# One row group of the output weight split over fewer DMA engines, and a shorter VectorE program, in a one-token decoder block

## The chip, the cores and the metric

The kernel runs on one core of a Trainium2 chip. The metric is device time in microseconds (us) for one execution. Below, "span" is the stretch that the hardware profiler records on the core, from its first to its last instruction; the device time is somewhat longer.

## The reference, cut to what matters

One token (a row of D = 1024 numbers) goes through an attention layer over a sliding window of a cache and, beside it, through a two-layer network; both start from the same normalised row, and the sum of both and of the input is the result.

```python
x  = A_x                                   # 1 x 1024
xn = layernorm(x)
# A: attention, 32 query heads, 4 key/value heads, the last W = 4096 of 65536 cache rows, Dh = 128
q  = (xn @ wq)                             # wq 1024 x 4096, 32 heads x 128
p  = softmax(q . k[-4096:] * 128**-0.5)    # 8 query heads share one k/v head
A  = (p @ v[-4096:]).reshape(4096) @ wo    # wo 4096 x 1024
# B: the network
h  = gelu(layernorm(xn) @ w1 + b1)         # w1 1024 x 3584
B  = h @ w2 + b2                           # w2 3584 x 1024
out = x + A + B                            # bf16, 1024 numbers
```

All inputs are bf16. Every weight and the used part of the cache are read once: k 4 MB, wq 8 MB, w1 7 MB, v 4 MB, w2 7 MB and wo 8 MB.

## The kernel before, in words

**Loads.** SyncE (SP) issues all large loads on one queue, in the order k_sb (4 pieces), wq (2), w1 (2), v_sb (3), w2 (2), wo (6 pieces, L228), and at the end the store of the result (L357). The tiles come from a ring of four 32 KB-per-partition buffers, so a load waits until the engines have finished with the tile that held its buffer. `wo` is seen as 128 partitions x 32 "rows": partition p holds the rows 32p to 32p+31 of the matrix, and row (or chunk) c of the kernel is the 128 x 1024 slab of row 32p+c over all p. The chunks 0 to 15 come with one load, the others with loads of 8, 4, 2, 1 and 1 chunks; the last two are chunk 30 and chunk 31.

**Start.** The input row is turned into a column by eight one-column matmuls (x_ps, L123); the two layer norms (L124 to L170) are a chain of small VectorE (DVE) instructions with matmuls against a matrix of ones for the sums and a power on GpSimd (POOL) for the reciprocal root. They give xnT and yT. DVE also zeroes the accumulators accq (L174) and acch (L246).

**Keys.** DVE transposes k in 32 x 32 blocks into kt_scr (L185, four instructions of 128 x 4096), and 64 copies of 32 x 1024 put the blocks in place in kT: 26 on ScalarE (ACT, L199), 38 on DVE (L201).

**TensorE (PE).** In order: q = xn @ wq into accq (L237); the first half of acch = y @ w1 (L257); the transpose of q (L261), which DVE copies into the mask tile qm (L266); the scores sp (L275); the second half of acch; softmax (L283 to L305); gelu (L312) and the transpose hT of its result (L314); o_all = p @ v (L319). DVE reduces o_all (L322, L324), casts it to o_bf (L326), and four matmuls with the selection matrix `spread` lay it out over 128 partitions as o8 (L329, L331), one column for each chunk of wo.

**End.** The rest is one long sum over 28 chunks of w2 (with hT) and 32 chunks of wo (with o8). All but the last TAIL = 8 chunks go into accf (L338), two matmuls of 512 columns a chunk. The last 8 go into another accumulator, acct (L353), four matmuls of 256 columns a chunk, one in each group of 32 columns of the array. When the last matmul into accf is done, four copies of 1 x 256 bring accf into the tile bulk, alternately on DVE (L348) and ACT (L350). They all write the same tile, and each waits for the one before it on the other engine. DVE then adds acct and bulk (res, L356), and SP stores res.

```python
    TAIL = 8
...
    for t in range(4):
        half, w = divmod(t, 2)
        src = accf[32 * half:32 * half + 1, 256 * w:256 * w + 256]
        if w == 0:
            nc.vector.tensor_copy(out=bulk[32 * t:32 * t + 1, :], in_=src)
        else:
            nc.scalar.copy(out=bulk[32 * t:32 * t + 1, :], in_=src)
```

The order on each engine is the order of the program; a scheduler moves independent instructions a little.

Of the kernel before, what the change touches and what calls it, by code (L numbers as in the profile page):

```python
# [16 lines left out]
def kernel(  # L17
# [21 lines left out]
    Hq = NQ // Dh  # L39
    REP = Hq // Hkv  # L40
    Fd = B_w1.shape[1]
    W = min(4096, max(256, Sk // 4))
    C = D // P
    NCH = W // P
    NJQ = NQ // 512
    WQ4 = W // 4
    CW2 = Fd // P
    CWO = NQ // P
    TAIL = 8
    NH = Fd // 8  # L50
    eps = 1e-5
# [3 lines left out]
    consts = ctx.enter_context(tc.tile_pool(name="consts", bufs=1))  # L55
# [28 lines left out]
    for i in range(2):  # L84
# [6 lines left out]

    ident = consts.tile([P, P], BF16)
# [3 lines left out]
    ones_f = consts.tile([P, P], FP32)  # L96
    nc.vector.memset(ones_f[:], 1.0)
    sel4 = consts.tile([P, Hq], FP32)
    ones_bf = consts.tile([P, 1], BF16)
    nc.vector.memset(ones_bf[:], 1.0)  # L100
    mhalf = consts.tile([P, 1], FP32)
    nc.vector.memset(mhalf[:], -0.5)
    dummy = consts.tile([1, 2], FP32)
    nc.scalar.activation(out=dummy[:, 0:1], in_=mhalf[0:1, 0:1], func=ACT.Exp)  # L104
    qm = consts.tile([P, Hkv, Hq], BF16)
    nc.gpsimd.memset(qm[:], 0.0)

# [3 lines left out]
                            pattern=[[-1, 4], [1, P]], channel_multiplier=-4)  # L111

# [11 lines left out]
    nc.vector.tensor_copy(out=xf[:], in_=x_ps[:])  # L124

    def layernorm(src_f32, dst_f32, dst_bf):
        n = float(P * C)
        st = small.tile([P, 1], FP32, tag="ln_st")
        nc.vector.reduce_sum(out=st[:], in_=src_f32, axis=AX.X)
# [8 lines left out]
        nc.vector.tensor_tensor(out=sq[:], in0=xc[:], in1=xc[:], op=ALU.mult)  # L138
        nc.vector.reduce_sum(out=st2[:], in_=sq[:], axis=AX.X)
# [6 lines left out]
        nc.vector.tensor_scalar_mul(out=dst_f32, in0=xc[:], scalar1=rstd[:])  # L146
        nc.vector.tensor_copy(out=dst_bf, in_=dst_f32)

    xn_f = consts.tile([P, C], FP32)
    xnT = consts.tile([P, C], BF16)  # L150
    layernorm(xf[:], xn_f[:], xnT[:])
    n_el = float(P * C)
    st12 = small.tile([P, 2], FP32, tag="ln2_st")
    nc.vector.reduce_sum(out=st12[:, 0:1], in_=xn_f[:], axis=AX.X)
    sq2 = small.tile([P, C], FP32, tag="ln2_sq")
    nc.vector.tensor_tensor(out=sq2[:], in0=xn_f[:], in1=xn_f[:], op=ALU.mult)
    nc.vector.reduce_sum(out=st12[:, 1:2], in_=sq2[:], axis=AX.X)
# [28 lines left out]
    nc.vector.tensor_reduce(out=sel4[:], in_=ident_f[:].rearrange("p (r h) -> p h r", r=4), axis=AX.X, op=ALU.add)  # L186
    act_share = [11, 8, 5, 2]
    act_moves, dve_moves = [], []
    for g in range(Hkv):
        T4 = scr[:, g, :].rearrange("p (c a j) -> p c a j", a=4, j=32)  # L190
        k = 0
        for R in range(4):
            for Cd in range(4):
                src = T4[32 * R:32 * R + 32, :, Cd, :]
                dst = kT[32 * Cd:32 * Cd + 32, g, WQ4 * R:WQ4 * (R + 1)].rearrange("p (c j) -> p c j", j=32)
                (act_moves if k < act_share[g] else dve_moves).append((dst, src))
                k += 1
    for (dst, src) in act_moves:
        nc.scalar.copy(out=dst, in_=src)  # L199
    for (dst, src) in dve_moves:  # L200
        nc.vector.tensor_copy(out=dst, in_=src)  # L201
# [44 lines left out]
    nc.vector.memset(acch[:], 0.0)  # L246
# [15 lines left out]
    for g in range(Hkv):  # L262
        b, th = divmod(g, 2)
        src = qT_ps[:, b * 4:(b + 1) * 4, 64 * th:64 * th + 64:32]
        dst = qm[:, g, g * REP:(g + 1) * REP].rearrange("p (t hh) -> p hh t", t=2)
        nc.vector.tensor_copy(out=dst, in_=src)  # L266
# [38 lines left out]
    nc.vector.tensor_scalar_mul(out=grs[:], in0=gmask[:], scalar1=rs[:])  # L305
# [4 lines left out]
    nc.vector.tensor_scalar_mul(out=zcol[:], in0=l_loc[:], scalar1=0.0)  # L310
# [30 lines left out]
    nc.vector.memset(acct[:], 0.0)  # L341
# [9 lines left out]
    for idx, (kind, c, wap) in enumerate(chunk_src[n_bulk:]):  # L351
        for t in range(4):
            nc.tensor.matmul(acct[32 * t:32 * t + 1, :], lhsT=vec[kind](c), rhs=wap[:, t * 256:(t + 1) * 256],  # L353
                             start=(idx == 0), stop=(idx == TAIL - 1), tile_position=(0, 32 * t))
# [33 lines left out]
```

## Time and profile before

| | |
|---|---|
| device time, median of 3 runs | 102.2 us (101.95 to 102.44) |
| device time of the profiled execution | 102.15 us |
| its span | 100.4 us |
| bytes read from HBM | 39.86 MB, 397 GB/s over the span |
| busy share: PE, DVE, ACT, POOL | 45%, 49%, 34%, 4% |
| DVE, ACT, POOL, PE matmul instructions | 91, 37, 17, 369 |
| instruction fetches seen inside the span | 3 of 16 KB, 1 of 8 KB |

In the profile, `PE` rows are matmuls and `PEld` rows are loads of the stationary operand; `L338` is line 338 of the kernel above; a bracket such as `[0.54 <-DMA wo...]` says how long the engine sat idle before the instruction and what ended that. `PEclk` is the TensorE clock that was granted, 1.00 being full speed. `SPq` is SP's issuing of DMAs. Times in the views run from the start of the span.

### The profile page before, as it was taken

What the parts mean: (1) busy time and instruction counts of PE and PEld (TensorE: products, weight loads), DVE (VectorE), ACT (ScalarE), POOL (GpSimd) and SP (SyncE); (2) the same over time, 40 slices, a digit from 0 to 9 for tenths busy, and PEclk for the clock granted to TensorE, in tenths of its full rate; (3) what the DMA queues carried; (4) which work ended last, traced back from release to release, by engine and by line L of the source; (5) the groups of instructions that cost most, each with busy time, mean ns of one, the idle gap of its engine ahead of it and who ended that gap; (6) DMA issues with size and microseconds to landing.
All of it is one profiled execution on the core that took longest, in us unless ns stands there. A gap on an engine that the chain in (4) does not pass through costs nothing.

```text
span 100.4 us, 976 instructions
## 1 busy us (share of the span) xinstructions
PE 45.7 (45%) x369; PEld 18.0 (18%) x369; DVE 49.2 (49%) x91; ACT 34.2 (34%) x37; POOL 4.0 (4%) x17
## 2 busy tenths in 40 slices
PE   0472000009500920297462009999199910299640
PEld 0422000003100300024221003334133400033210
DVE  4616799999999999992552460000900000000310
ACT  2300008999999999902204630000000000000100
POOL 6024200000000000000000000000000000000000
PEclk9999999999999997559999655589957995559975
DMA  2999999999999998999999998989989999999900
GB/s 40 375 431 434 499 431 496 431 418 418 418 418 392 468 440 369 502 400 400 390 440 424 424 506 388 509 377 423 480 388 414 418 444 437 437 405 401 382 33 1
DMA packets 2882, 39.92 MB, mean 397 GB/s; under 512 B 311, under 2 KB 315, under 8 KB 702
## 3 DMA queue, kind: packets, MB, share of 16 engines
q1 hardware_dynamic: 2872, 39.85, 93.3%
q8 instruction: 3, 0.05, 0.2%
q10 hardware_dynamic: 6, 0.01, 0.0%
q14 instruction: 1, 0.01, 0.0%
HBM read 39.86 MB, written 0.00 MB: 397 GB/s over the span
## 4 chain that ended last, share of the span: by engine, by line
DVE 39%; DMA 25%; PE 15%; issue 8%; ACT 5%; POOL 3%; SPq 2%; POOLq 1%; ACTq 0%; DVEq 0%
DMA wo<-in_A_wo_dram 25%; DVE kt_scr L185 17%; DVE kT L201 16%; PE o_all L319 10%; PE sp L275 2%; DVE hT L314 2%; SPq L228 2%; PE acch L257 2%; ACT L312 1%; ACT e L297 1%; DVE eTb L299 1%; DVE m_loc L283 1%; ACT h_sb L312 1%; DVE q_sb L240 1%; POOLq L383 1%
## 5 line engine op out<-in xcount | busy, mean ns | idle before, releaser
L199 ACT COPY kT<-kt_scr 32x1024 bf16<-32x1024 bf16 x26 | 27.1, 1042 | 12.2 <-DVE kt_scr L185 12.0
L185 DVE STREAM_TRANSPOSE kt_scr<-k_sb 128x4096 bf16<-128x4096 bf16 x4 | 17.4, 4409 | 0.0
L201 DVE COPY kT<-kt_scr 32x1024 bf16<-32x1024 bf16 x38 | 15.9, 419 | 0.5
L237 PE MATMUL accq<-wq,xnT 128*1 128x512 bf16 x64 | 6.9, 607 | 19.5 <-DMA wq<-in_A_wq_dram 19.5
L350 ACT COPY bulk<-accf 1x256 f32<-1x256 f32 x2 | 0.7, 361 | 36.3 <-DVE bulk L348 36.3
L319 PE MATMUL o_all<-v_sb,eTb 128*32 128x512 bf16 x32 | 9.9, 484 | 5.4 <-DVE hT L314 5.4
L348 DVE COPY bulk<-accf 1x256 f32<-1x256 f32 x2 | 0.8, 416 | 21.6 <-PE accf L338 21.1
L338 PE MATMUL accf<-wo,o 128*1 128x512 bf16 x48 | 6.8, 449 | 6.5 <-DMA wo<-in_A_wo_dram 6.5
L338 PE MATMUL accf<-w,hT 128*1 128x512 bf16 x56 | 8.1, 452 | 0.1
L257 PE MATMUL acch<-w,yT 128*1 128x448 bf16 x64 | 4.8, 463 | 6.3 <-DMA w<-in_B_w_dram 6.3
L237 PEld LDWEIGHTS <-xnT 128*1 128x1 bf16 x64 | 2.1, 116 | 23.8 <-issue 23.8
L319 PEld LDWEIGHTS <-eTb 128*32 128x32 bf16 x32 | 3.7, 117 | 11.2 <-DVE hT L314 5.5
L322 DVE TENSOR_TENSOR o_m<-o_all,grs 32x512 f32<-32x512 f32 x1 | 0.7, 679 | 10.0 <-PE o_all L319 10.0
L338 PEld LDWEIGHTS <-o 128*1 128x1 bf16 x48 | 2.4, 94 | 10.9 <-issue 8.8
L338 PEld LDWEIGHTS <-hT 128*1 128x1 bf16 x56 | 2.8, 96 | 4.9 <-issue 2.7
L257 PEld LDWEIGHTS <-yT 128*1 128x1 bf16 x64 | 1.7, 99 | 9.0 <-issue 8.3
L314 DVE STREAM_TRANSPOSE hT<-h_sb 128x896 bf16<-128x896 bf16 x1 | 1.7, 1699 | 2.4 <-ACT h_sb L312 2.4
L297 ACT ACTIVATE e<-sc,nmx 128x1024 bf16<-128x1024 f32 x1 | 1.1, 1147 | 3.9 <-DVE nmx L294 3.9
L353 PE MATMUL acct<-wo,o 128*1 128x256 bf16 x32 | 1.7, 283 | 1.7 <-DMA wo<-in_A_wo_dram 1.7
L275 PE MATMUL sp<-kT,qm 128*32 128x512 bf16 x32 | 2.1, 380 | 0.3 <-DVE qm L266 0.3
L104 ACT ACT_TABLE_LOAD x1 | 1.3, 1283 | 1.9 <-issue 1.9
L299 DVE STREAM_TRANSPOSE eTb<-e 128x1024 bf16<-128x1024 bf16 x1 | 1.2, 1246 | 1.4 <-ACT e L297 1.4
(85 smaller groups left out, 32.2 us busy)
## 6 DMA issues: line engine op xcount, KB each, us to landing
w<-in_B_w_dram SPq DMA_DIRECT2D x4, 3584.0 KB, 23.7
wq<-in_A_wq_dram SPq DMA_DIRECT2D x2, 4096.0 KB, 19.9
k_sb<-in_A_k_cache_dram SPq DMA_DIRECT2D x4, 1024.0 KB, 7.0
wo<-in_A_wo_dram SPq DMA_DIRECT2D x1, 4096.0 KB
v_sb<-in_A_v_cache_dram SPq DMA_DIRECT2D x1, 2048.0 KB
v_sb<-in_A_v_cache_dram SPq DMA_DIRECT2D x2, 1024.0 KB, 22.5
wo<-in_A_wo_dram SPq DMA_DIRECT2D x1, 2048.0 KB, 21.6
wo<-in_A_wo_dram SPq DMA_DIRECT2D x1, 1024.0 KB
```

The lines of the kernel that those rows point to most:

```text
L185: nc.vector.transpose(out=scr[:, g, :], in_=k2[:, g, :])
L199: nc.scalar.copy(out=dst, in_=src)
L201: nc.vector.tensor_copy(out=dst, in_=src)
L228: nc.sync.dma_start(out=tv[:, a:b, :], in_=wo_v[:, nr * i + a:nr * i + b, :])
L237: nc.tensor.matmul(accq[32 * t:32 * t + 1, b, :], lhsT=xnT[:, c:c + 1], rhs=w3[:, r, j * 512:(j + 1) * 512], start=(c == 0), stop=(c == C ...
L257: nc.tensor.matmul(acch[32 * t:32 * t + 1, b, :NH], lhsT=yT[:, c:c + 1], rhs=w3[:, r, j * NH:(j + 1) * NH], start=False, stop=(c == C - 1) ...
L275: nc.tensor.matmul(sp[32 * R:32 * R + 32, :], lhsT=qm[:, g, :], rhs=kT[:, g, c0:c0 + 512], start=(g == 0), stop=(g == Hkv - 1), tile_posit ...
L297: nc.scalar.activation(out=e128[:], in_=sc[:], func=ACT.Exp, bias=nmx[:], scale=scale, accum_out=l_loc[:])
L299: nc.vector.transpose(out=eTb[:], in_=e128[:])
L314: nc.vector.transpose(out=hT[:], in_=h_sb[:].rearrange("p (d c) -> p c d", c=CW2))
L319: nc.tensor.matmul(o_all[:].rearrange("h g d -> h (g d)"), lhsT=eTb[:, 32 * c:32 * c + 32], rhs=v4[:, :, c, :], start=(c == 0), stop=(c == ...
L338: nc.tensor.matmul(accf[32 * half:32 * half + 1, :], lhsT=vec[kind](c), rhs=wap[:, half * 512:(half + 1) * 512], start=False, stop=(idx == ...
```

## The change

It has two parts.

First, chunk 30 of wo is no longer loaded by one DMA of 128 partitions. Its 128 slab rows are loaded by three DMAs: 48 rows to partitions 32 to 79 of the ring tile (wo_m), 48 rows to partitions 32 to 79 of a new tile wo_x, and 32 rows to partitions 0 to 31 of the ring tile. The source of each has 12, 12 or 8 as its outer dimension and 4 as its inner. Partitions 0 to 31 of wo_x are zeroed by POOL. Chunk 30 is then multiplied in two parts of 80 partitions each (8 matmuls instead of 4), and o8 gets two more columns, made by 8 one-column matmuls with a second selection matrix spread_x, that hold the matching order of o. TAIL becomes 4: accf takes 28 chunks of wo, acct four.

Second, DVE's 91 instructions become 44 (four of them only read out an accumulated sum). The 38 DVE copies into kT become 10, each over all four k/v heads (32 x 4 x 1024), and ACT does 24 copies, six of each head. The four copies into qm become 2, the four copies of the row maximum become part of one reduction, several sums are taken as the accumulated output of the instruction before, and memsets, casts, small products and zeroings move to POOL or ACT. POOL has 32 instructions instead of 17 (its first ones now also make the constants), ACT has a few more.

```diff
-    TAIL = 8
+    TAIL = 4
...
-        nc.vector.tensor_copy(out=dst_bf, in_=dst_f32)
+        nc.scalar.copy(out=dst_bf, in_=dst_f32)
...
-    nc.vector.tensor_tensor(out=msq2[:], in0=mean2[:], in1=mean2[:], op=ALU.mult)
+    nc.gpsimd.tensor_tensor(out=msq2[:], in0=mean2[:], in1=mean2[:], op=ALU.mult)
...
-    nc.vector.tensor_tensor(out=ve2[:], in0=ve2[:], in1=msq2[:], op=ALU.subtract)
+    nc.gpsimd.tensor_tensor(out=ve2[:], in0=ve2[:], in1=msq2[:], op=ALU.subtract)
...
+    MOVED = 30
+    moves = ((0, 32, 12, 0), (1, 32, 12, 48), (0, 0, 8, 96))
+    spread_x = consts.tile([Hq, 2, 4, P], BF16)
+    nc.gpsimd.memset(spread_x[:], 0.0)
+    for s, m0, ne, p0 in moves:
+        sx = spread_x[:, s, :, m0:m0 + 4 * ne].rearrange("h q (e v) -> h q e v", e=ne)
+        nc.gpsimd.affine_select(out=sx, in_=sx, compare_op=ALU.not_equal, fill=1.0, base=p0,
+                                pattern=[[-1, 4], [1, ne], [ne, 4]], channel_multiplier=-4)
+    wo_x = consts.tile([80, D], BF16)
+    nc.gpsimd.memset(wo_x[0:32, :], 0.0)
...
-    nc.vector.memset(accq[:], 0.0)
+    nc.scalar.mul(accq[:].rearrange("p b n -> p (b n)"), mhalf[:].to_broadcast([P, 1024]), 0.0)
...
-    act_share = [11, 8, 5, 2]
+    act_share = [6, 6, 6, 6]
...
+    for k, (R, Cd) in enumerate(pairs):
+        g0 = sum(k < share for share in act_share)
+        if g0 < Hkv:
+            nc.vector.tensor_copy(out=kT[32 * Cd:32 * Cd + 32, g0:, WQ4 * R:WQ4 * (R + 1)].rearrange("p g (c j) -> p g c j", j=32),
+                                  in_=T5[32 * R:32 * R + 32, g0:, :, Cd, :])
...
-            nc.sync.dma_start(out=tv[:, a:b, :], in_=wo_v[:, nr * i + a:nr * i + b, :])
+            if nr * i + a != MOVED:
+                nc.sync.dma_start(out=tv[:, a:b, :], in_=wo_v[:, nr * i + a:nr * i + b, :])
+                continue
+            wo_m = tv[0:80, a, :]
+            for s, m0, ne, p0 in moves:
+                rows = A_wo[p0 * CWO:(p0 + 4 * ne) * CWO, :].rearrange("(v e c) n -> e v c n", e=ne, c=CWO)
+                nc.sync.dma_start(out=(wo_m, wo_x)[s][m0:m0 + 4 * ne, :], in_=rows[:, :, MOVED, :])
...
-    nc.vector.memset(acch[:], 0.0)
+    nc.scalar.mul(acch[:].rearrange("p b n -> p (b n)"), mhalf[:].to_broadcast([P, 1024]), 0.0)
...
-    nc.vector.tensor_copy(out=o_bf[:], in_=o_f[:])
+    nc.scalar.copy(out=o_bf[:], in_=o_f[:])
...
+    for s in range(2):
+        for q in range(4):
+            nc.tensor.matmul(o8_ps[:, 32 + s:33 + s], lhsT=spread_x[:, s, q, :], rhs=o_bf[:, 32 * q + MOVED:32 * q + MOVED + 1],
+                             start=(q == 0), stop=(q == 3))
...
-        for t in range(4):
-            nc.tensor.matmul(acct[32 * t:32 * t + 1, :], lhsT=vec[kind](c), rhs=wap[:, t * 256:(t + 1) * 256],
-                             start=(idx == 0), stop=(idx == TAIL - 1), tile_position=(0, 32 * t))
+        parts = [(vec[kind](c), wap)]
+        if kind == "o" and c == MOVED:
+            parts = [(o8[0:80, 32:33], wo_m), (o8[0:80, 33:34], wo_x)]
+        for (lh, rh) in parts:
+            for t in range(4):
+                nc.tensor.matmul(acct[32 * t:32 * t + 1, :], lhsT=lh, rhs=rh[:, t * 256:(t + 1) * 256],
+                                 start=(idx == 0), stop=(idx == TAIL - 1), tile_position=(0, 32 * t))
```

More of the change, by code (lines that the diff above doesn't have):

```diff
@@ L89 @@
     kt_scr = ring_tile("kt_scr")
+    mhalf = consts.tile([P, 1], FP32)
+    nc.gpsimd.memset(mhalf[:], -0.5)
+    ones_bf = consts.tile([P, 1], BF16)
+    nc.gpsimd.memset(ones_bf[:], 1.0)
+    ones_f = consts.tile([P, P], FP32)
+    nc.gpsimd.memset(ones_f[:], 1.0)
     ident = consts.tile([P, P], BF16)
@@ L95 @@
     make_identity(nc, ident_f[:])
-    ones_f = consts.tile([P, P], FP32)
-    nc.vector.memset(ones_f[:], 1.0)
     sel4 = consts.tile([P, Hq], FP32)
[L99 to L102, printed above, removed]
     dummy = consts.tile([1, 2], FP32)
     nc.scalar.activation(out=dummy[:, 0:1], in_=mhalf[0:1, 0:1], func=ACT.Exp)
-    qm = consts.tile([P, Hkv, Hq], BF16)
+    qm = consts.tile([P, Hkv * (Hq + REP)], BF16)
     nc.gpsimd.memset(qm[:], 0.0)
-    spread = consts.tile([Hq, 4, P], BF16)
-    nc.gpsimd.memset(spread[:], 0.0)
-    nc.gpsimd.affine_select(out=spread[:], in_=spread[:], compare_op=ALU.not_equal, fill=1.0, base=0,
-                            pattern=[[-1, 4], [1, P]], channel_multiplier=-4)
-    gmask = consts.tile([Hq, Hkv], FP32)
-    nc.gpsimd.memset(gmask[:], 1.0)
-    nc.gpsimd.affine_select(out=gmask[:], in_=gmask[:], compare_op=ALU.is_ge, fill=0.0, base=0,
-                            pattern=[[-REP, Hkv]], channel_multiplier=1)
-    nc.gpsimd.affine_select(out=gmask[:], in_=gmask[:], compare_op=ALU.is_ge, fill=0.0, base=REP - 1,
-                            pattern=[[REP, Hkv]], channel_multiplier=-1)
     xf = consts.tile([P, C], FP32)
@@ L123 @@
         nc.tensor.matmul(x_ps[:, c:c + 1], lhsT=xb2[0:1, c:D:C], rhs=ones_bf[0:1, 0:1], start=True, stop=True)
-    nc.vector.tensor_copy(out=xf[:], in_=x_ps[:])
+    st = small.tile([P, 1], FP32, tag="ln_st")
+    nc.vector.tensor_scalar(out=xf[:], in0=x_ps[:], scalar1=1.0, scalar2=None, op0=ALU.mult, op1=ALU.add, accum_out=st[:])
+    st12 = small.tile([P, 2], FP32, tag="ln2_st")
     def layernorm(src_f32, dst_f32, dst_bf):
         n = float(P * C)
-        st = small.tile([P, 1], FP32, tag="ln_st")
-        nc.vector.reduce_sum(out=st[:], in_=src_f32, axis=AX.X)
         tot = ps_f.tile([P, 1], FP32, tag="pf", name="ln_tot")
@@ L137, in layernorm @@
         st2 = small.tile([P, 1], FP32, tag="ln_st2")
-        nc.vector.tensor_tensor(out=sq[:], in0=xc[:], in1=xc[:], op=ALU.mult)
-        nc.vector.reduce_sum(out=st2[:], in_=sq[:], axis=AX.X)
+        nc.vector.scalar_tensor_tensor(out=sq[:], in0=xc[:], scalar=1.0, in1=xc[:], op0=ALU.mult, op1=ALU.mult, accum_out=st2[:])
         tot2 = ps_f.tile([P, 1], FP32, tag="pf", name="ln_tot2")
@@ L145, in layernorm @@
         nc.gpsimd.tensor_tensor(out=rstd[:], in0=ve[:], in1=mhalf[:], op=ALU.pow)
-        nc.vector.tensor_scalar_mul(out=dst_f32, in0=xc[:], scalar1=rstd[:])
-        nc.vector.tensor_copy(out=dst_bf, in_=dst_f32)
+        nc.vector.tensor_scalar(out=dst_f32, in0=xc[:], scalar1=rstd[:], scalar2=None, op0=ALU.mult, op1=ALU.add,
+                                accum_out=st12[:, 0:1])
+        nc.scalar.copy(out=dst_bf, in_=dst_f32)
     xn_f = consts.tile([P, C], FP32)
@@ L152 @@
     n_el = float(P * C)
-    st12 = small.tile([P, 2], FP32, tag="ln2_st")
-    nc.vector.reduce_sum(out=st12[:, 0:1], in_=xn_f[:], axis=AX.X)
     sq2 = small.tile([P, C], FP32, tag="ln2_sq")
-    nc.vector.tensor_tensor(out=sq2[:], in0=xn_f[:], in1=xn_f[:], op=ALU.mult)
-    nc.vector.reduce_sum(out=st12[:, 1:2], in_=sq2[:], axis=AX.X)
+    nc.vector.scalar_tensor_tensor(out=sq2[:], in0=xn_f[:], scalar=1.0, in1=xn_f[:], op0=ALU.mult, op1=ALU.mult,
+                                   accum_out=st12[:, 1:2])
     tot12 = ps_f.tile([P, 2], FP32, tag="pf", name="ln2_tot")
@@ L170 @@
     nc.vector.tensor_scalar(out=yT[:], in0=xn_f[:], scalar1=mean2[:], scalar2=rstd2[:], op0=ALU.subtract, op1=ALU.mult)
+    spread = consts.tile([Hq, 4, P], BF16)
+    nc.gpsimd.memset(spread[:], 0.0)
+    nc.gpsimd.affine_select(out=spread[:], in_=spread[:], compare_op=ALU.not_equal, fill=1.0, base=0,
+                            pattern=[[-1, 4], [1, P]], channel_multiplier=-4)
+    MOVED = 30
[8 more added lines that the diff above has]
+    nc.gpsimd.memset(wo_x[0:32, :], 0.0)
+    gmask = consts.tile([Hq, Hkv], FP32)
+    nc.gpsimd.memset(gmask[:], 1.0)
+    nc.gpsimd.affine_select(out=gmask[:], in_=gmask[:], compare_op=ALU.is_ge, fill=0.0, base=0,
+                            pattern=[[-REP, Hkv]], channel_multiplier=1)
+    nc.gpsimd.affine_select(out=gmask[:], in_=gmask[:], compare_op=ALU.is_ge, fill=0.0, base=REP - 1,
+                            pattern=[[REP, Hkv]], channel_multiplier=-1)
     accf = ps_acc.tile([P, 512], FP32, tag="accf")
     accq = ps_acc.tile([P, 2, 512], FP32, tag="accq", name="accq")
-    nc.vector.memset(accq[:], 0.0)
+    nc.scalar.mul(accq[:].rearrange("p b n -> p (b n)"), mhalf[:].to_broadcast([P, 1024]), 0.0)
     for half in range(2):
@@ L185 @@
         nc.vector.transpose(out=scr[:, g, :], in_=k2[:, g, :])
-    nc.vector.tensor_reduce(out=sel4[:], in_=ident_f[:].rearrange("p (r h) -> p h r", r=4), axis=AX.X, op=ALU.add)
-    act_share = [11, 8, 5, 2]
-    act_moves, dve_moves = [], []
-    for g in range(Hkv):
[L190 to L201, printed above, removed]
+    nc.gpsimd.tensor_tensor(out=sel4[:], in0=ident_f[:, 0:Hq], in1=ident_f[:, Hq:2 * Hq], op=ALU.add)
+    for r in range(2, 4):
+        nc.gpsimd.tensor_tensor(out=sel4[:], in0=sel4[:], in1=ident_f[:, r * Hq:(r + 1) * Hq], op=ALU.add)
+    act_share = [6, 6, 6, 6]
+    T5 = kt_scr[:].rearrange("p (g c a j) -> p g c a j", g=Hkv, a=4, j=32)
+    pairs = [(R, Cd) for R in range(4) for Cd in range(4)]
+    for g in range(Hkv):
+        for (R, Cd) in pairs[:act_share[g]]:
+            nc.scalar.copy(out=kT[32 * Cd:32 * Cd + 32, g, WQ4 * R:WQ4 * (R + 1)].rearrange("p (c j) -> p c j", j=32),
+                           in_=T5[32 * R:32 * R + 32, g, :, Cd, :])
+    for k, (R, Cd) in enumerate(pairs):
[3 more added lines that the diff above has]
+                                  in_=T5[32 * R:32 * R + 32, g0:, :, Cd, :])
     for i in range(2):
@@ L261 @@
             nc.tensor.transpose(qT_ps[:, b * 4 + hh, :], q_sb[:, b, hh * Dh:(hh + 1) * Dh], ident[:])
[L262 to L265, printed above, removed]
+    for b in range(2):
+        src = qT_ps[:, b * 4:(b + 1) * 4, :].rearrange("p hh (th t j) -> p th hh t j", th=2, t=2)[:, :, :, :, 0]
+        dst = qm[:].rearrange("p (b th r) -> p b th r", b=2, th=2)[:, b, :, 0:REP].rearrange("p th (t hh) -> p th hh t", t=2)
         nc.vector.tensor_copy(out=dst, in_=src)
@@ L274 @@
                 c0 = WQ4 * R + 512 * a
-                nc.tensor.matmul(sp[32 * R:32 * R + 32, :], lhsT=qm[:, g, :], rhs=kT[:, g, c0:c0 + 512],
+                nc.tensor.matmul(sp[32 * R:32 * R + 32, :], lhsT=qm[:, Hq * g:Hq * (g + 1)], rhs=kT[:, g, c0:c0 + 512],
                                  start=(g == 0), stop=(g == Hkv - 1), tile_position=(0, 32 * R))
@@ L285 @@
     nc.tensor.transpose(mT_ps[:], m_loc[:], ident_f[:])
-    m_row = small.tile([1, Hq], FP32, tag="m_row")
-    nc.vector.tensor_reduce(out=m_row[:], in_=mT_ps[:].rearrange("a (r h) -> a h r", r=4), axis=AX.X, op=ALU.max)
     m_rep = small.tile([1, 4, Hq], FP32, tag="m_rep")
-    for R in range(4):
-        nc.vector.tensor_copy(out=m_rep[:, R, :], in_=m_row[:])
+    m_in = mT_ps[:].rearrange("a (r h) -> a h r", r=4).unsqueeze(1).to_broadcast([1, 4, Hq, 4])
+    nc.vector.tensor_reduce(out=m_rep[:], in_=m_in, axis=AX.X, op=ALU.max)
     mc_ps = ps_f.tile([P, 1], FP32, tag="pf", name="mc_ps")
@@ L304 @@
     grs = small.tile([Hq, Hkv], FP32, tag="grs")
-    nc.vector.tensor_scalar_mul(out=grs[:], in0=gmask[:], scalar1=rs[:])
+    nc.gpsimd.tensor_scalar_mul(out=grs[:], in0=gmask[:], scalar1=rs[:])
     h_sb = consts.tile([P, 2 * NH], BF16)
     zcol = small.tile([P, 1], FP32, tag="zcol")
-    nc.vector.tensor_scalar_mul(out=zcol[:], in0=l_loc[:], scalar1=0.0)
+    nc.gpsimd.tensor_scalar_mul(out=zcol[:], in0=l_loc[:], scalar1=0.0)
     for b in range(2):
@@ L325 @@
     o_bf = consts.tile([Hq, Dh], BF16)
-    nc.vector.tensor_copy(out=o_bf[:], in_=o_f[:])
-    o8_ps = ps_f.tile([P, 32], FP32, tag="pf", name="o8_ps")
+    nc.scalar.copy(out=o_bf[:], in_=o_f[:])
+    o8_ps = ps_f.tile([P, 34], FP32, tag="pf", name="o8_ps")
     for q in range(4):
-        nc.tensor.matmul(o8_ps[:], lhsT=spread[:, q, :], rhs=o_bf[:, 32 * q:32 * q + 32], start=(q == 0), stop=(q == 3))
-    o8 = consts.tile([P, 32], BF16)
+        nc.tensor.matmul(o8_ps[:, 0:32], lhsT=spread[:, q, :], rhs=o_bf[:, 32 * q:32 * q + 32], start=(q == 0), stop=(q == 3))
+    for s in range(2):
+        for q in range(4):
+            nc.tensor.matmul(o8_ps[:, 32 + s:33 + s], lhsT=spread_x[:, s, q, :], rhs=o_bf[:, 32 * q + MOVED:32 * q + MOVED + 1],
+                             start=(q == 0), stop=(q == 3))
+    o8 = consts.tile([P, 34], BF16)
     nc.vector.tensor_copy(out=o8[:], in_=o8_ps[:])
@@ L340 @@
     acct = ps_f.tile([P, 256], FP32, tag="pf", name="acct")
-    nc.vector.memset(acct[:], 0.0)
+    nc.scalar.mul(acct[:], mhalf[:].to_broadcast([P, 256]), 0.0)
     bulk = consts.tile([97, 256], FP32)
```

## The prediction

> **What bounds the kernel now.** I read the slices of the page first, to see what is busy to the end.
>
> ```profile
> PE   0472000009500920297462009999199910299640
> DVE  4616799999999999992552460000900000000310
> PEclk9999999999999997559999655589957995559975
> DMA  2999999999999998999999998989989999999900
> ```
>
> The DMA engines are full from the second slice to two slices before the end; no compute engine is. DVE is full in the first 45 us only. The chain of waits says what that leaves at the end:
>
> ```profile
> 72.14 24.75 DMA wo<-in_A_wo_dram
> 96.93 0.41 PE acct L353 x3
> 97.43 0.42 DVE res L356
> ```
>
> The last load ends the kernel; behind it come 0.50 us to the start of res and then res and the store. The timeline of the last 4 us shows each of the last loads' arrivals, and a second chain beside them:
>
> ```profile
> 93.95 0.41 DVE L348 COPY bulk<-accf 1x256 f32<-1x256 f32 x1 [21.11 <-PE accf L338]
> 94.45 0.61 PE L353 MATMUL acct<-wo,o 128*1 128x256 bf16 x16 [0.54 <-DMA wo<-in_A_wo_dram]
> 94.46 0.36 ACT L350 COPY bulk<-accf 1x256 f32<-1x256 f32 x1 [35.84 <-DVE bulk L348]
> 94.85 0.42 DVE L348 COPY bulk<-accf 1x256 f32<-1x256 f32 x1 [0.48 <-ACT bulk L350]
> 95.30 0.36 ACT L350 COPY bulk<-accf 1x256 f32<-1x256 f32 x1 [0.48 <-DVE bulk L348]
> 96.29 0.28 PE L353 MATMUL acct<-wo,o 128*1 128x256 bf16 x4 [0.22 <-DMA wo<-in_A_wo_dram]
> 96.93 0.38 PE L353 MATMUL acct<-wo,o 128*1 128x256 bf16 x4 [0.36 <-DMA wo<-in_A_wo_dram]
> ```
>
> Chunks 24 to 27 arrive at 94.45, chunk 30 at 96.29, chunk 31 at 96.93. The four copies of accf run one after another, 93.95 to 95.66 (95.30 + 0.36), 1.71 us in all, and are done 1.8 us before res needs them. They start when the last matmul into accf ends.
>
> Why does chunk 31 arrive so late? In the trace's single DMA packets its 16 completion writes (one of each engine) come at 95.08 to 95.47 from thirteen engines, and at 95.90, 96.43 and 96.60 from three. The three were level until instruction fetches came in: for wq's last load all 16 are within 0.41 us. A fetch of 16 KB takes 0.93 us at 37.1, one of 8 KB 0.31 us at 38.2, another of 16 KB 0.94 us at 64.0; after each, one more engine is behind and stays so. (A third of 16 KB, at 95.5, finds its engine done.) On a late engine the eight 2 KB packets of chunk 30 and their completion take 0.65 us (completions at 95.95 and 96.60). PE starts 0.33 us after the last write.
>
> **Part one, chunk 30.** What the trace does not show is where the new DMAs run. Nearest rows: the store of 4 rows makes 4 packets with 4 completions, the load of one row one packet with one, every load of 128 partitions 16 completions. So a short DMA uses no more engines than rows. Between 16 engines with 3 + 3 + 2 packets each, where every engine still has eight (gain nothing), and the outer sizes 12, 12 and 8, where eight engines get 12 packets, four get 8 and four none, I take the second, since the source is ordered in just these outer sizes and 4 rows went to 4 engines. The Trainium skill, "DMA: Bandwidth & Descriptors", section "Why a DMA increments its semaphore by 16 and not by 1", says that the count is the largest number up to 16 dividing the outer sizes of both sides, and that the lowest-numbered engines are taken; by it engines 12 to 15 are spared and the sum is the same. Its "Rules for kernel authors" warn of just such an outer size under 16, as it confines a DMA to fewer engines; by that alone the load would be slower by the four packets of the next paragraph.
>
> If the late engines are among the four spared, the latest ends at 96.60 - 0.65 = 95.95, the next at 95.78; the 8 KB fetch may go altogether, as DVE's program shrinks. The engines with 12 packets end at 95.47 + 4 x 0.08 = 95.79. So chunk 31 is there for PE at 96.93 - 0.65 = 96.28, and acct would let res start at 96.28 + 0.50 = 96.78 instead of 97.43. If the late ones are among those with 12, they end 0.33 us later instead.
>
> **TAIL = 4.** Chunks 24 to 27 move from acct to accf. They are there for PE at 94.45, as set by the same late engines, whose earlier loads do not change. Eight matmuls of 512 columns run two at a time, a pair in 0.216 us at full clock: 3 x 0.216 + 0.38 for the last = 95.48. DVE starts 0.04 later (93.91 to 93.95 before), 95.52; the four copies take their 1.71 us to 97.23; 0.03 to the next engine, and res starts at 97.26. That is later than 96.78: the copies take the place of the load as what ends last. Sum: 97.43 - 97.26 = 0.17 us gained, of 0.65 that the loads give. All behind res is unchanged, so 102.15 - 0.17 = 101.98 against the profiled execution, which lies 0.05 under the median; I say 102.0.
>
> **What the clock does to it.** That chain now holds PE's pace, which the copies' 1.8 us of slack hid before. The windows:
>
> ```profile
> 60.43:66.15 5.72, 5.72 (x14) 2.00 (x15) 0.00 (x0) 0.00 (x0) 0.00 (x0) 0.50 1.00 429
> 66.15:70.31 4.16, 4.16 (x19) 1.72 (x18) 0.00 (x0) 0.00 (x0) 0.00 (x0) 1.00 1.01 434
> 87.15:90.05 2.90, 2.90 (x14) 0.88 (x15) 0.00 (x0) 0.00 (x0) 0.00 (x0) 0.50 1.00 429
> 90.05:93.91 3.86, 3.86 (x36) 1.40 (x32) 0.00 (x0) 0.00 (x0) 0.00 (x0) 1.00 0.98 410
> ```
>
> (The last three columns are granted clock, DMA share and GB/s.) PE starts from a wait at half clock; it got full clock after 5.72 us at 60.43 and after 2.90 us at 87.15. A pair takes 0.427 us before and 0.216 after. Chunks 0 to 23 are 24 pairs from 87.15: with 2.90 us at half clock they end at 93.76, before chunk 24 arrives. With 4.3 us they end just at 94.45. With 5.72: 13.4 pairs, then 10.6 x 0.216 = 2.29, to 95.16, and everything behind it is 0.71 later: res at 97.97, 0.54 after now. Before, that cost nothing: copies from 95.36 to 97.07, still ahead of 97.43. The Trainium skill, "TensorE: Matmul & The Clock Gate", section "Part 1: The HAM clock gate", states that activity is judged in free-running windows of 3.4 us, so that the delay changes from run to run; no view of one execution can show that, but the two delays above differ by 2.8 us.
>
> **Part two, DVE.** It ends its busy stretch at 44.7 and everything that hangs on it has cover: PE waits 6.47 us for wo's first load at 87.15 ("[6.47 <-DMA wo...]"). Removed: 38 copies x 0.419 = 15.9 us. Added: 10 copies of four times the size. Upper bound, no saving: 10 x 4 x 0.419 = 16.8. Lower, with 0.158 (qm's 8-element copy) as the fixed part paid once instead of four times: 10 x (0.158 + 4 x 0.261) = 12.0. I take 12.0, nearest in kind; neither matters. ACT's copies: 24 x 1.042 = 25.0 instead of 27.1.
>
> In the norms, DVE saves five instructions of 0.16 and one of 0.56 (xnT, now ACT's), but the second norm gets two POOL steps of about 0.55 (the power, L168, took 0.553) behind memsets of about 0.5 and 1.0 (L109, 0.514, doubled) and a selection of 0.63. yT, and with it the transposes, could come from 0.6 earlier to 2 us later; I take 1.1 later. Behind them on SP waits w1's second load, issued at 28.6 now; the loads queued ahead of it last until about 40, so that is hidden too. The zeroing of accq and acch on ACT, bounded by 1.15 us each (the exponential of 128x1024), follows the table load and ends by 5.8; PE needs acch at 6.65, with the second sum of the norm queued behind it. Without that cover it would cost what it overran, inside the same 2 us. o_bf on ACT, the eight small matmuls and grs, zcol on POOL cost at most 1 us before 73, inside the 6.47. The three new DMAs are issued near 72, more than 20 us ahead of their turn. So part two is worth nothing unless the cover of 6.47 us is used up.
>
> **Rivals.**
>
> *The load's gain comes through whole.* Then the copies would have to end by 96.78: they would have to overlap. Both engines' brackets show them waiting for each other, and the changed program keeps those waits. 102.15 - 0.65 = 101.5.
>
> *Slower: PE is still slow when chunk 24 comes.* Place: L338's last pairs, price 0.51 us for each us of half clock beyond 4.3. It turns gain into loss at 4.65 us and passes 0.5% at 5.7. At 5.72: 102.7. For it: the row at 60.43. Against: the row at 87.15 itself, 2.90, and the median damps it.
>
> *The rows are not spared where it counts.* Late engines not among the four: acct at 97.43 as now or up to 97.76: 102.15 to 102.5, no change by the measure below.
>
> *The big copies lose the fast form.* At over 2.2 us each (against 1.2 to 1.7) kT comes 6.5 us later and the cover is gone; no row points there. From 102.2 upwards.
>
> **How the numbers follow.** Half a percent, 0.51 us, is about what can be told from no change. Copies last, with the clock as it comes: 0.62, at 101.8 to 102.6. Rows not spared: 0.13, 102.1 to 102.5. Gain whole: 0.08, 101.5. Clock late in the typical run too: 0.13, about 102.7. Big copies or another loss of cover: 0.04. Faster 0.08, slower 0.17, the rest 0.75. The range 101.7 to 102.7 takes in the first two and most of the fourth.
>
> **What would show it.** Right: PE's last wait for wo ends near 96.3 and the page's chain ends with bulk copies, the first at 95.5, before res at 97.2 to 97.4; DVE's large copies 1.2 us each; transposes near 12; one fetch fewer. Wrong: res waits for acct; chunk 31 no earlier than 96.9; PE not idle for 4 us or more before wo.

## The result, and the profile after

| | before | after |
|---|---|---|
| device time, median | 102.2 us (101.75 to 102.44, 8 runs) | 102.75 us (102.36 to 103.14, 8 runs) |
| ratio | | 1.0057 (95%: 1.0042 to 1.0072) |
| span, median | 100.5 us (33 further runs) | 100.6 us (100.2 to 101.0) |
| device time less span, median | 1.74 us (33 further runs) | 2.15 us (2.07 to 2.26) |
| profiled execution: device time, span | 102.15, 100.4 us | 102.97, 100.9 us |

The change makes the kernel 0.55 us slower (102.75 - 102.2). The forecast was 102.0 with a range to 102.7, so the time lies just outside it. By the forecast's own half percent (0.51 us) the kernel is slower, by a hair, and the case that was given 0.75, no change, did not come.

The fourth row of the table holds the largest part of it: some 0.4 us lie behind or ahead of the span, where none of the views used in the forecast shows any work. The rest is in the last 4 us of the span, so that is where the views are to be read first. The chain of waits of the changed kernel (start and length in us, then what):

```profile
54.56 32.73 DMA wo<-in_A_wo_dram
...
87.33 8.84 PE accf L352 x56
96.17 0.02 issue
96.20 0.42 DVE bulk L362
96.62 0.02 issue
96.64 0.37 ACT bulk L364
...
97.49 0.37 ACT bulk L364
97.86 0.02 issue
97.88 0.42 DVE res L374
```

Before, the chain went from the last load over acct to res at 97.43. Now the load that releases it is wo's first one; PE's sum into accf and the four copies set the end, as the forecast had it, but res starts at 97.88 and not at 97.26. The windows by clock say why (PE busy time and instructions, PEld's, DVE's, ACT's, POOL's, then clock, DMA share, GB/s):

```profile
87.33:92.65 5.32, 5.32 (x26) 1.66 (x27) 0.00 (x0) 0.00 (x0) 0.00 (x0) 0.50 0.99 421
92.65:96.20 3.55, 3.55 (x42) 1.49 (x40) 0.00 (x1) 0.00 (x0) 0.00 (x0) 1.00 0.79 312
```

PE ran at half clock for 5.32 us behind its wait, not for 2.90. And the timeline of the end shows that the load would not have allowed much either:

```profile
95.86 0.62 PE L371 MATMUL acct<-wo,o 128*1 128x256 bf16 x12
96.53 0.28 PE L371 MATMUL acct<-wo_x,o 80*1 80x256 bf16 x4
97.16 0.28 PE L371 MATMUL acct<-wo,o 128*1 128x256 bf16 x4 [0.35 <-DMA wo<-in_A_wo_dram]
```

Chunk 31 is there for PE at 97.16; before it was 96.93, and the forecast said 96.28. In the trace's single packets the last completion writes end at 96.78 and 96.80 (96.44 and 96.61 before).

The middle of the kernel went as forecast; from the costliest groups (count, then busy us and mean ns, then idle before):

```profile
L193 DVE STREAM_TRANSPOSE kt_scr<-k_sb 128x4096 bf16<-128x4096 bf16 x4 | 17.4, 4405 | 0.0
L207 DVE COPY kT<-kt_scr 32x4096 bf16<-32x4096 bf16 x10 | 12.2, 1220 | 0.2
L352 PE MATMUL accf<-wo,o 128*1 128x512 bf16 x56 | 8.8, 490 | 6.5 <-DMA wo<-in_A_wo_dram 6.5
```

Ten large copies take 1.22 us each, and PE still waits 6.47 us for wo at 87.33. Last, the list of DMA queues, of after:

```profile
q1 hardware_dynamic: 2888, 39.85, 93.0%
q8 instruction: 3, 0.05, 0.2%
q10 hardware_dynamic: 6, 0.01, 0.0%
```

The three fetches of 16 KB are there (0.05 MB in three packets); the page before had a fourth line, `q14 instruction: 1, 0.01, 0.0%`, the fetch of 8 KB at 38.2 us. It is gone from the span. The forecast had counted that as a gain or as nothing.

### The profile page after: what moved, and what is told of

Its sections match the earlier page's. It is cut to its first block, busy times and chain, and to the rows that moved or that the text cites. A ratio compares the mean times of both kernels' runs of the same rounds, so it can differ in the third digit from the quotient of the medians.

```text
span 100.9 us, 964 instructions
## 1 busy us (share of the span) xinstructions
PE 47.9 (47%) x373; PEld 19.0 (19%) x373; DVE 41.5 (41%) x44; ACT 34.7 (34%) x40; POOL 9.4 (9%) x32
## 4 chain that ended last, share of the span: by engine, by line
DMA 68%; PE 21%; DVE 3%; SPq 2%; ACT 1%; issue 1%
DMA wo<-in_A_wo_dram 32%; DMA wq<-in_A_wq_dram 20%; DMA w<-in_B_w_dram 16%; PE accf L352 9%; PE acch L270 6%; PE accq L250 4%; PE sp L287 2%; SPq L73 2%; DVE m_loc L295 1%; DVE bulk L362 1%; ACT bulk L364 1%; DVE m_rep L300 1%; ACT sc L292 1%; PE qT_ps L274 1%; DVE res L374 0%
## 5 line engine op out<-in xcount | busy, mean ns | idle before, releaser
L202 ACT COPY kT<-kt_scr 32x1024 bf16<-32x1024 bf16 x24 | 25.0, 1042 | 8.2 <-DVE kt_scr L193 8.0
L329 PE MATMUL o_all<-v_sb,eTb 128*32 128x512 bf16 x32 | 9.4, 469 | 5.9 <-DMA v_sb<-in_A_v_cache_dram 5.9
L207 DVE COPY kT<-kt_scr 32x4096 bf16<-32x4096 bf16 x10 | 12.2, 1220 | 0.2
L352 PE MATMUL accf<-wo,o 128*1 128x512 bf16 x56 | 8.8, 490 | 6.5 <-DMA wo<-in_A_wo_dram 6.5
L270 PE MATMUL acch<-w,yT 128*1 128x448 bf16 x64 | 6.0, 553 | 6.3 <-DMA w<-in_B_w_dram 6.3
L352 PEld LDWEIGHTS <-o 128*1 128x1 bf16 x56 | 2.9, 102 | 12.3 <-issue 10.5
L156 DVE TENSOR_SCALAR yT<-xn_f,mean,rstd 128x8 bf16<-128x8 f32 x1 | 2.1, 2081 | 2.2 <-POOL rstd L154 2.2
L292 ACT COPY sc<-sp 128x512 f32<-128x512 f32 x1 | 0.6, 586 | 5.7 <-PE sp L287 5.7
```

Source lines behind the costliest of these rows:

```text
L202: nc.scalar.copy(out=kT[32 * Cd:32 * Cd + 32, g, WQ4 * R:WQ4 * (R + 1)].rearrange("p (c j) -> p c j", j=32), in_=T5[32 * R:32 * R + 32, g, ...
L207: nc.vector.tensor_copy(out=kT[32 * Cd:32 * Cd + 32, g0:, WQ4 * R:WQ4 * (R + 1)].rearrange("p g (c j) -> p g c j", j=32), in_=T5[32 * R:32 ...
L270: nc.tensor.matmul(acch[32 * t:32 * t + 1, b, :NH], lhsT=yT[:, c:c + 1], rhs=w3[:, r, j * NH:(j + 1) * NH], start=False, stop=(c == C - 1) ...
L329: nc.tensor.matmul(o_all[:].rearrange("h g d -> h (g d)"), lhsT=eTb[:, 32 * c:32 * c + 32], rhs=v4[:, :, c, :], start=(c == 0), stop=(c == ...
L352: nc.tensor.matmul(accf[32 * half:32 * half + 1, :], lhsT=vec[kind](c), rhs=wap[:, half * 512:(half + 1) * 512], start=False, stop=(idx == ...
```

## The experiments

Theory: the loss is made of (1) time outside the span that comes with the short DVE program, some 0.4 us, and (2) the copies of accf behind a PE that is often still at half clock, 0.1 to 0.2 us in the median; (3) the three loads of chunk 30 gain and lose in different executions, nothing in the middle. Part (1) was formed when the DVE part alone had run. Rivals: the time outside comes from POOL's longer program or from the new tiles and loads; the three loads themselves are the loss; the late DMA engines are always the same.

| kernel | median us | ratio to before (95%) | span, median (range) | outside, median |
|---|---|---|---|---|
| changed kernel | 102.75 | 1.0057 (1.0042 to 1.0072) | 100.6 (100.2 to 101.0) | 2.15 |
| DVE part alone | 102.52 | 1.0027 (1.0017 to 1.0036) | 100.4 (100.2 to 100.5) | 2.17 |
| DVE part + 46 memsets | 102.13 | 0.9998 (0.9986 to 1.0010) | 100.4 (100.1 to 100.7) | 1.75 |
| DVE part + 23 memsets | 102.07 | 0.9990 (0.9980 to 1.0001) | 100.35 (100.2 to 100.6) | 1.73 |
| DVE part + 4 memsets | 102.41 | 1.0012 (0.9998 to 1.0027) | 100.45 (100.3 to 100.6) | 2.01 |
| before + 20 POOL memsets | 102.21 | 1.0003 (0.9989 to 1.0016) | 100.4 (100.2 to 100.8) | 1.76 |
| before, TAIL = 4 | 102.37 | 1.0020 (1.0000 to 1.0040) | 100.6 (100.3 to 101.3) | 1.79 |
| the same, PE kept busy | 102.27 | 1.0012 (1.0001 to 1.0023) | 100.55 (100.4 to 100.8) | 1.75 |
| before, chunk 30 in 3 loads | 102.23 | 0.9995 (0.9976 to 1.0013) | 100.45 (99.9 to 100.9) | 1.74 |
| before, chunk 30 in 4 loads | 102.54 | 1.0058 (1.0031 to 1.0085) | 100.8 (100.6 to 101.7) | 1.75 |
| changed, TAIL = 8 | 102.68 | 1.0028 (1.0006 to 1.0049) | 100.5 (99.8 to 100.8) | 2.13 |
| changed, TAIL = 8, + 46 memsets | 102.19 | 1.0000 (0.9984 to 1.0017) | 100.4 (100.0 to 101.0) | 1.76 |
| changed + 46 memsets | 102.34 | 1.0006 (0.9991 to 1.0020) | 100.6 (100.2 to 100.9) | 1.75 |

"Outside" is the device time of each execution less its span. Each ratio is against runs of the kernel before on the same chip; it weighs all executions, so it can leave the medians where the executions fall into two groups (102.54 and 102.68 in the table). The kernels ran on several chips, on which the median of the kernel before is 102.16 to 102.22.

### TAIL alone

```diff
-    TAIL = 8
+    TAIL = 4
```

on the kernel before.

> The kernel before with TAIL = 4 and nothing else. Theory A (the loss is the chain of bulk copies, which TAIL = 4 puts behind chunks 24 to 27 and behind PE's pace): res follows the copies, at 97.3 us with an early clock and up to 98.0 with a late one; device time 102.0 to 102.8, in the middle 102.4. Theory B (the loss lies outside the recorded span, where the changed kernel has 2.1 us and the profiled execution before had 1.75): no change, 102.2, and 1.75 us outside the span. Theory C (the late DMA engines were not spared, and the loads end as late as before): by itself it predicts no change here.

Its timeline at the end:

```profile
96.25 0.41 DVE L348 COPY bulk<-accf 1x256 f32<-1x256 f32 x1 [23.75 <-PE accf L338]
97.06 0.28 PE L353 MATMUL acct<-wo,o 128*1 128x256 bf16 x4 [0.32 <-DMA wo<-in_A_wo_dram]
...
97.59 0.36 ACT L350 COPY bulk<-accf 1x256 f32<-1x256 f32 x1 [0.49 <-DVE bulk L348]
97.99 0.43 DVE L356 TENSOR_TENSOR res<-acct,bulk 97x256 bf16<-97x256 f32 x1 [0.43 <-ACT bulk L350]
```

Full clock came at 92.76 here, and res at 97.99 waits for ACT's copy, 0.53 us later than chunk 31 would have let it start (97.06 + 0.40, as from 96.50 to res at 96.90 below). That is the forecast's slower rival, 97.97 for 5.72 us of half clock. Over twelve executions the spans spread from 100.3 to 101.3, where the kernel before has 100.3 to 100.8: a median cost of 0.1 to 0.2 us, whose interval begins at no change (1.0000), and a tail of four executions at 101.0 or more.

### The same with PE kept busy

```diff
+    warm = ps_tp.tile([32, 512], FP32, tag="tp", name="warm")
     for idx, (kind, c, wap) in enumerate(chunk_src[:n_bulk]):
...
+        if idx == CW2:
+            for i in range(26):
+                nc.tensor.matmul(warm[:], lhsT=o8[:], rhs=kT[:, 0, 0:512], start=True, stop=True)
```

26 matmuls whose result is not used stand between the chunks of w2 and those of wo.

> The kernel before with TAIL = 4 and 26 matmuls of 512 columns whose result is thrown away, between the two halves of the w2 sum, so that PE comes to wo's first load at full clock. If the spread of TAIL = 4 (spans of 100.3 to 101.3) is PE's late clock: full clock from 87.2 on, bulk copies from 95.5 to 97.2 in every run, spans of 100.2 to 100.5, median 102.05. If the copies are late for another reason (the arrival of chunks 24 to 27): spans as with TAIL = 4 alone, up to 101.3, 102.4.

Its windows and the end of its timeline:

```profile
76.66:86.80 10.14, 9.75 (x64) 4.04 (x61) 0.00 (x0) 0.00 (x0) 0.00 (x0) 1.00 1.01 435
86.80:94.50 7.70, 5.51 (x48) 2.09 (x48) 0.00 (x0) 0.00 (x0) 0.00 (x0) 1.00 0.97 407
```

```profile
94.73 1.03 PE L342 MATMUL accf<-wo,o 128*1 128x512 bf16 x8 [0.56 <-DMA wo<-in_A_wo_dram]
...
97.14 0.36 ACT L354 COPY bulk<-accf 1x256 f32<-1x256 f32 x1 [0.48 <-DVE bulk L352]
97.23 0.28 PE L357 MATMUL acct<-wo,o 128*1 128x256 bf16 x4 [0.37 <-DMA wo<-in_A_wo_dram]
97.63 0.42 DVE L360 TENSOR_TENSOR res<-acct,bulk 97x256 bf16<-97x256 f32 x1 [0.52 <-PE acct L357]
```

With the clock at 1.00 throughout, the last pairs no longer wait for PE but for chunk 24 (94.73), the copies end at 97.50, and res waits for acct again. The spread of the spans shrinks from 1.0 to 0.4 us: the longest executions came from the clock. The median missed its forecast: 102.27 and not 102.05, with spans up to 100.8 and not 100.5. In this profile the last load is what ends, as it did before, and it ends later: the third fetch of 16 KB comes at 91.36 us, under the loads, and no longer at 95.5, and chunk 31's last completion write ends at 96.89 (96.61 before). So the added matmuls may have a cost of their own. The interval overlaps that of TAIL = 4 without them, and the clock's share of the median cost is not settled by these two.

### Chunk 30 in three loads, alone

The change's part one with the old DVE program and TAIL = 8: `moves`, `spread_x`, `wo_x`, the three loads, two more columns of o8 and `parts`, as in the diff of the change.

> The kernel before with chunk 30's load split over 12, 12 and 8 engines, TAIL = 8 and the old DVE program. Prediction's sum, with the late engines spared: chunk 31 for PE at 96.3 and a device time of 101.55. Theory C: the late engines still do eight packets of chunk 30, chunk 31 for PE at 96.9 or later, 102.2. Theory B, if the three odd loads or the longer PE program cause it: 2.1 us outside the span and 102.55.

The end of the profiled execution:

```profile
96.17 0.28 PE L378 MATMUL acct<-wo_x,o 80*1 80x256 bf16 x4
96.20 0.36 ACT L371 COPY bulk<-accf 1x256 f32<-1x256 f32 x1 [0.48 <-DVE bulk L369]
96.50 0.28 PE L378 MATMUL acct<-wo,o 128*1 128x256 bf16 x4
96.90 0.42 DVE L381 TENSOR_TENSOR res<-acct,bulk 97x256 bf16<-97x256 f32 x1 [0.73 <-PE acct L378]
```

In this execution chunk 31 is there at 96.50, res starts 0.53 us earlier than before (97.43 to 96.90), and the span is 99.9: the forecast's gain of the load, nearly whole. But the median of twelve is no different from before. The completion writes of single engines suggest the reason. In this execution the two engines that were latest before chunk 30 took no part in it, and their last writes end at 96.04 and 96.11; the very last, at 96.14, is that of a third, less late engine, which carried 12 packets of it. In the changed kernel's profile both late engines did 4 + 4 of its packets, just the eight they had before (one of them ends the load before at 95.48, the two parts of chunk 30 at 95.80 and 96.13, and chunk 31 at 96.78). So which engines are late is not the same in the two profiles; sparing some does not help when the late ones are others. That it also differs between executions of one kernel is inferred from its spans, 99.9 to 100.9 here.

### Chunk 30 in four loads of 8 x 4

```diff
-    moves = ((0, 32, 12, 0), (1, 32, 12, 48), (0, 0, 8, 96))
+    moves = ((0, 0, 8, 0), (0, 32, 8, 32), (0, 64, 8, 64), (0, 96, 8, 96))
```

on the kernel before (no wo_x; chunk 30 is one product of 128 partitions again). Eight engines then do 16 packets each and eight none.

> The kernel before (TAIL = 8, old DVE program) with chunk 30 loaded by four DMAs with outer size 8 and inner size 4, all four to the ring tile: eight engines do 16 packets of it and eight none. If the engines that serve the instruction fetches are always among those spared by 12, 12, 8, both late ones are spared here too, and the load ends with the eight others, 0.5 us earlier than before: spans of 100.0, 101.7. If they differ from execution to execution, two kinds of runs: about a quarter near 100.0, the others with a late engine that carries 16 packets, 0.6 us longer than before, spans of 101.1; median 102.7 or more.

```profile
96.50 0.65 PE L376 MATMUL acct<-wo,o 128*1 128x256 bf16 x12 [1.19 <-DMA wo<-in_A_wo_dram]
97.39 0.28 PE L376 MATMUL acct<-wo,o 128*1 128x256 bf16 x4 [0.23 <-DMA wo<-in_A_wo_dram]
```

Of its twelve spans eight are 100.6 to 100.8 and four 101.3 to 101.7. Were the late engines always among the eight that are used, all would be near the upper group. Two groups in one kernel speak for places that differ by execution. The expected fast group, near 100.0, did not come: in its profile eight engines' last writes end at 96.06 to 96.56 and two more at 96.62 and 96.94, where thirteen engines of the kernel before were done by 95.48, so even a spared late engine would gain little. Part of that is a slow stretch: from 95.2 to 95.9 us packets of 2 KB took up to 0.167 us, where 0.084 is usual in this trace. Why, and how the places are chosen, stays open.

### The DVE part alone, and filled up again

The change's part two alone (the rewritten DVE, POOL and ACT instructions; chunk 30 in one load, TAIL = 8):

> The changed kernel without the split of chunk 30 and with TAIL = 8, so the shorter DVE program alone. Theory A: nothing on the path, 102.2. Theory B, if the longer POOL program or the moved instructions cause it: the span unchanged (100.4), 2.1 us outside it, 102.55. Also one late engine fewer, since the fetch of 8 KB goes.

Span 100.4, as before; time 0.3 us longer; outside 2.17 us. In its profile res starts where it did (97.43 before):

```profile
97.44 0.42 DVE L349 TENSOR_TENSOR res<-acct,bulk 97x256 bf16<-97x256 f32 x1 [1.81 <-PE acct L346]
```

So the rewritten instructions cost nothing that the span shows, and the loss is outside. The same kernel with DVE's program brought back to its old length by one-element memsets, all of which run in the first 4 us, and the opposite, the kernel before with POOL's program lengthened:

```diff
+    pad = consts.tile([1, 64], FP32)
+    for i in range(46):
+        nc.vector.memset(pad[:, i:i + 1], 0.0)
```

```diff
+    pad = consts.tile([1, 64], FP32)
+    for i in range(20):
+        nc.gpsimd.memset(pad[:, i:i + 1], 0.0)
```

> The shorter DVE program alone (TAIL = 8, whole load of chunk 30), with 46 one-element memsets added on DVE, so that DVE's program is as long as before, and POOL's as long as in the changed kernel. If the 0.4 us outside the span come from DVE's program having become short, they go: 1.74 us outside, 102.15, and the 8 KB instruction fetch is back in the middle of the span. If they come from POOL's longer program, or from the work that was moved, they stay: 2.15 outside, 102.5 and no such fetch of DVE's.

> The kernel before with 20 one-element memsets added on POOL, so that POOL's program is as long as in the changed kernel, DVE's as before. If POOL's length makes the 0.4 us outside the span: 2.15 outside, 102.6. If DVE's does: 1.74 outside, 102.2. The memsets delay the second norm by about 1 us, which is hidden either way.

46 instructions that compute nothing make the kernel faster by 0.3 to 0.4 us (102.52 to 102.13; against the kernel before on each one's chip, +0.31 and -0.03), and outside falls from 2.17 to 1.75. POOL's length does nothing. With 23 and with 4 memsets instead of 46:

> The rewritten DVE program alone (TAIL = 8, one load for chunk 30) with 23 added memsets instead of 46: 67 instructions in all. In the two longer programs the 8 KB fetch came when DVE had done about 50 and 60 instructions. Theory (either the fetch is reached inside the span or it is not): the fetch shows in the span, later than 13.7 us, since the 50th to 60th instruction now comes at 41 to 72 us; device time less span is 1.75 and the time 102.1 to 102.2. Rival (the time outside goes down in proportion to the program's length): 2.17 less half of 0.42, so 1.96, and the time 102.35.

> The same with only 4 added memsets: 48 instructions in all, fewer than the 50 after which the 8 KB fetch came in the long programs. Theory (reached or not): no 8 KB fetch in the span, device time less span 2.15 as without the memsets, the time 102.5. Rival (in proportion to the length): 2.17 less 4/46 of 0.42, so 2.13, which cannot be told from 2.15; the run tells the two apart only together with the one of 23 memsets. Rival (any memset ahead of the first real instruction does it, whatever the length): 1.75 and 102.15.

With 23 the fetch is in the span, at 52.7 us, in its list of DMA queues:

```profile
q14 instruction: 1, 0.01, 0.0%
```

Outside is 1.73: not half of the 0.4 us is left but none of it. With 4 the profiled execution has no such fetch inside its span of 100.3 us; but the list of DMA queues for the stretch from 100 to 110 us, all but 0.3 us of it behind the span, has one packet:

```profile
DMA packets 1, 0.01 MB, mean 1 GB/s; under 512 B 0, under 2 KB 0, under 8 KB 0
## 3 DMA queue, kind: packets, MB, share of 16 engines
q14 instruction: 1, 0.01, 0.2%
```

It starts at 102.35, 2.01 us behind the end of the span (100.34), and takes 0.31 us. By its size and queue it is taken here for the fetch that comes and goes with DVE's length, though the same queue also carries six or seven packets of 8 KB ahead of the span. Then this short program has that fetch too, only behind the span: a program long enough takes it under the loads (when the 50th, 58th and 61st DVE instruction had begun, with 91, 67 and 90 in all).

That the late fetch is what costs the 0.4 us fits, but is not shown. In this execution all of the time outside the span is 2.02 us, so the packet starts about when that time is over, if all of it lies behind the span; where device time begins and ends around the span is not recorded. In the traces of the changed kernel and of the DVE part alone no packet is recorded behind the span. Nor do the semaphore events there tell the kernels apart: the last one lies 1.90 us behind the span in the kernel before, in the changed kernel and in the DVE part alone, while 1.72, 2.12 and 2.12 us lie outside. What the runs show is the length: the short DVE program has 0.4 us more outside, and added instructions take them away.

With 48 instructions neither forecast came, 2.13 or 2.15 outside: the ten executions run from 1.69 to 2.13, with 2.01 in the middle, so this length stands at the edge. The rival by which any memset does it, whatever the length, is not borne out by the middle either.

The Trainium skill, "Runtime: NRT & Kernel Launch", section "Instruction fetch mechanics", says that the instruction memory is refilled in blocks of 16 KiB and that the cost of crossing into the next is mostly hidden. Here the fetch that goes with DVE's program is one packet of 8 KB. Under the loads it is hidden here too (spans of 100.4 us with it and without it); whether one at the end is, stays open as said.

### Both undone in the changed kernel

> The changed kernel with TAIL = 8. Theory A: the copies are hidden again and res waits for the last load: with the late engines not spared a span of 100.4 to 100.5, so 0.2 to 0.3 under the changed kernel's 102.75 in the middle. Theory B: 2.1 us outside the span as in the changed kernel. A and B together: 102.5; A alone: 102.2; B alone: 102.75.

With TAIL = 8 alone single spans go down to 99.8, but the median span is 100.5 (100.6 in the changed kernel), and outside stays at 2.13: 102.68, where 102.5 was expected. With the memsets, then with both:

> The whole change (TAIL = 4, chunk 30 in three loads, the short DVE program), with 46 one-element memsets added to DVE's program, which run before its first real instruction. Theory (the short DVE program costs 0.41 us outside the recorded span, and the rest of the loss is TAIL = 4): the 8 KB fetch comes back inside the span, device time less span is 1.75 (2.15 in the changed kernel), the span stays near 100.6, and the time is 102.75 - 0.40 = 102.35. Rival (the time outside the span comes from the three loads, the new tiles or the longer POOL program too): device time less span 1.9 or more, and the time 102.5 or more.

> The same with TAIL = 8, so that the copies have their slack back. Theory: device time less span 1.75; the span as with TAIL = 8 and the three loads in the kernel before, 100.45; the time 102.68 - 0.40 = 102.28 or a little under, no difference from the kernel before (102.2). Rival (the rewritten DVE program and the three loads cost something in the span together): the span 100.7 or more and the time 102.5 or more.

102.34 against an expected 102.35, and 102.19 against 102.28. The 46 memsets alone bring the changed kernel from 0.55 to 0.12 us above the kernel before, from which it can then not be told; with TAIL = 8 too nothing is left. The rewritten DVE program and the three loads cost nothing together inside the span. None of the kernels can be told to be faster than before; the lowest, 102.07 with 23 memsets, has 1 inside its interval.

## Why the prediction was wrong

By its own steps:

**All behind res is unchanged.** This step failed, and with it "part two is worth nothing". The sum went from 97.43 to the device time as if all that follows were fixed. Inside the span it is (3.0 us from res to the end, before and after); outside it is not: 2.15 us instead of 1.74. Of the 0.77 us between forecast and result (102.75 - 101.98), 0.4 is this term, the largest; most of the rest is the span, which was to become 0.17 shorter and became 0.1 longer in the median. The runs showed in its place that a short DVE program alone costs 0.4 us outside the span (2.17, and 1.75 with 46 added memsets). The fetch of 8 KB was in the working, and its going was counted only as an engine less behind; where it would go to was not asked. Whether the fetch itself makes the 0.4 us stays open.

**TAIL = 4.** The mechanism was right: copies last, chunk 31 no longer the bound. The forecast's formula gives the profile: its price for each us beyond 4.3, 0.49 by its own paces of 0.427 and 0.216 (not 0.51), is 0.50 for 5.32 us; PE started 0.18 later (87.33); the copies took 1.65 (96.20 to 97.85) instead of 1.71. 97.26 + 0.50 + 0.18 - 0.06 = 97.88, as measured. Mis-sized was how often: 0.13 for a late clock in the typical run. The delays in the profiles were 2.90 before and 5.32 after; over the profiles of all thirteen kernels without the added matmuls they run from 2.90 to 5.94 us, and eight lie above 4.3. The trace's clock changes only at distances of whole multiples of 3.41 us (3.41, 6.83 and 10.24), in step with the free-running windows that the Trainium skill, "TensorE: Matmul & The Clock Gate", section "Part 1: The HAM clock gate", gives; so one row of 2.90 was no evidence for the next execution's.

**Chunk 30.** The confinement was right: the trace has 324 completion writes after and 308 before, and 12 + 12 + 8 - 16 is the 16 more. (The 0.65 us was read off chunk 31's eight packets, 95.95 to 96.60; chunk 30's on that engine took as long.) That most of the gain of 0.65 us of the load can be had was right for single executions (res 0.53 earlier in one, spans of 99.8 and 99.9). Wrong was to take the late engines of one profile for those of every execution: "rows not spared", with 0.13, is what both late engines of the changed kernel's profile show, and the gain in the median over executions is zero. With TAIL = 4 the copies end later than the load, so that a gain of the load does not count.

**Part two's work.** Right: large copies 1.2 us, transposes from 11.31 (near 12 was forecast), the cover of 6.47 us intact, one fetch fewer in the span. Its inside cost is nothing, as the DVE part alone shows (100.4).

**The sum as it came.** Against before's median of 102.2: +0.4 outside, +0.1 to 0.2 by TAIL = 4 (not clear of noise), 0 by the three loads and by the rewriting, together 102.7 to 102.8; measured 102.75. The rival that ended slower gave the same time (102.7), but by luck: its mechanism, PE's late clock, explains about a quarter of the loss (0.1 to 0.2 of 0.55).

## What to carry to other kernels

Device time has a part that the span does not show; when instructions are taken away, compare device time less span too, and look where the instruction fetches lie before and after. A gain that depends on which DMA engines are late needs more than one execution behind it, and a chain that is moved from a load onto PE inherits PE's clock as it comes. When one execution's row (2.90 us here, with 5.72 beside it in the same profile) decides between gain and loss, give both rows the same weight.

## What the runs showed of the hardware that was not expected

- A DVE program of 44 instructions has some 0.4 us more outside the span than one of 67 to 91 (2.13 to 2.17 against 1.73 to 1.79 us); 23 one-element memsets take all of it away, as 46 do. With 48 instructions the executions lie between the two levels and on both (1.69 to 2.13).
- A packet of 8 KB, taken for the fetch that goes with DVE's program, was recorded 2.01 us behind the end of a span. At which instruction that fetch is due was not measured (50, 58 and 61 begun when it came in three long programs).
- The DMA engines that end late are not the same in every profile: chunk 31's last write came at 96.14 to 96.94 in the profiles of the kernels with a split chunk 30. In the earliest the two latest engines had no work in chunk 30, in the changed kernel's (96.80) both had. What decides it stays open.
